# Moving four more k1 to Pool and reordering the loads around the first x of a fused FFT filter and feed-forward kernel

## The chip, the cores and the metric

The kernel runs on one core of one Trainium2 chip. The metric is the device time of one execution in microseconds (us); lower is better. Executions of one kernel agree within about 0.3%. A core has five engines that matter here: PE (TensorE, matmuls), DVE (VectorE), ACT (ScalarE), POOL (GpSimd) and SP (SyncE, which here only issues transfers), and 16 DMA engines. "PEld" in the profile is PE's weight load. In this kernel PE writes its results to banks of PSUM, a memory of the core, and VectorE or ScalarE brings them from there to the working memory, SBUF; this is called evacuation below.

## The reference

For each of 8 batches a sequence of 3008 positions with 256 channels is filtered in frequency, and the result goes through a two-layer feed-forward block:

```python
X = np.fft.rfft(x, axis=1)                      # x: (8, 3008, 256)
Y = X * (filt_r + 1j * filt_i)[None, :, :]
y = np.fft.irfft(Y, n=3008, axis=1)
h = y.reshape(24064, 256) @ w_in                # 256 -> 2048
out = np.maximum(0.01 * h, h) @ w_out           # 2048 -> 256
```

## The kernel before

The FFT is done by matmuls: 3008 = 94 x 32, so a first stage multiplies by a 94-point matrix, VectorE transposes, a second stage multiplies by one matrix for each of 24 frequencies k1 (`f2_sb`, three parts of 8), the filters are multiplied in, and two inverse stages follow (`inv2`, `i1_sb`). Later batches are woven into the feed-forward matmuls. The first batch has nothing to be woven into; its own code, the head, works on two halves of 128 channels.

```python
nc.sync.dma_start(small_sb[:], small_d.ap())
first_parts = ((0, 10), (10, 10), (20, 8), (28, 4))
for n0, nn in first_parts:
    x_load(0, n0, nn)                          # issued by Pool, float32 to float16 on the way
for hf in range(2):
    filt_load(fa_sb, filt_r, hf * DH, DH)      # two transfers each, issued by Pool
    filt_load(fb_sb, filt_i, hf * DH, DH)
    for i in (1, 0, 2) if hf == 0 else ():
        nc.gpsimd.dma_start(f2_sb[:, ts(i, NC // FP), :], f2_d.ap()[i])
nc.gpsimd.dma_start(w_in_sb[:], ...)
# ...
def first_s2(hf, c, n, kind, on_pool=False):   # second stage for k1 c to c+n-1
    ps = bank(kind, n, DH)                     # "pf": one of three PSUM banks, "ph": of two wide ones
    # ... n matmuls with f2_sb ...
    if on_pool:
        # act copies PSUM to SBUF (xs), which Pool reads
        # then 2 x n/4 products of 128x512 on gpsimd
    else:
        for i in range(2):
            nc.vector.tensor_tensor(y[i], ps, fs[i], AL.mult)
# ...
keep_warm(14)                                  # matmuls on zeros, meant to keep PE's clock up
# first stage, part by part of x, copies by dve and act in turn
t1_part(0, 0, True)(), t1_part(0, 1, True)()
upper(0, fa_sb, act), upper(0, fb_sb, dve)     # copy filters to the upper 64 partitions
first_s2(0, 8, 8, "ph", True)
t1_part(0, 2, True)()
first_s2(0, 0, 8, "ph")
# ... i1 load, next x load, t1_part(0, 3), upper(1, ...), and so on: see the diff
```

`upper(hf, fb_sb, dve)` copies one half of fb to the other partitions, on VectorE, and needs that half's filter loads; the products on VectorE stand behind it in program order.

Of the kernel before, what the change touches and what calls it, by code (L numbers as in the profile page):

```python
# [10 lines left out]
P = 128  # L11
# [8 lines left out]
NC = 24  # L20
Q = 32
R1 = 96
FP = 3
# [46 lines left out]
def kernel(  # L70
# [9 lines left out]
    nc = tc.nc  # L80
# [12 lines left out]
    f2_d = nc.inline_tensor(f2_np, name="fwd2_const")  # L93
# [4 lines left out]
    f2_sb = cpool.tile([P, NC, P], FP16, name="f2_sb")  # L98
    i1_sb = cpool.tile([P, N2, N1], FP16, name="i1_sb")
    small_sb = cpool.tile([P, 3, P], FP16, name="small_sb")  # L100
    fa_sb = cpool.tile([P, NC, D], FP16, name="fa_sb")
    fb_sb = cpool.tile([P, NC, D], FP16, name="fb_sb")
    w_in_sb = cpool.tile([P, NDT, DFF], FP16, name="w_in_sb")
# [17 lines left out]
    def bank(kind, n, w):  # L121
        of = wide if kind == "ph" else single
        t = of[turn[kind] % len(of)]
        turn[kind] += 1
        return t[:, : n * w].rearrange("p (n w) -> p n w", n=n)
# [5 lines left out]
    DH = D // 2  # L131

    def x_load(b, n0=0, nn=N2, d0=0, dn=D):

        for lo, cnt in ((0, R1),) if b + 1 < B else ((0, 64), (64, N1 - 64)):
            nc.gpsimd.dma_start(  # L136
                x_sb[lo : lo + cnt, ds(n0, nn), ds(d0, dn)],
                bass.AP(tensor=x.tensor, offset=x.offset + (b * N + lo * N2 + n0) * D + d0,
                        ap=[[N2 * D, cnt], [D, nn], [1, dn]]))

    def filt_load(dst, src, d0, dn):

        for q, first, sgn in ((0, 0, 1), (Q, N1, -1)):
            nc.gpsimd.dma_start(
                dst[q : q + Q, :, ds(d0, dn)],
                bass.AP(tensor=src.tensor, offset=src.offset + first * D + d0,
                        ap=[[N1 * D, N2 // 2], [sgn * NC * D, 2], [sgn * D, NC], [1, dn]]))


    nc.sync.dma_start(small_sb[:], small_d.ap())  # L150
    first_parts = ((0, 10), (10, 10), (20, 8), (28, 4))
    for n0, nn in first_parts:
        x_load(0, n0, nn)
    for hf in range(2):
        filt_load(fa_sb, filt_r, hf * DH, DH)
        filt_load(fb_sb, filt_i, hf * DH, DH)
        for i in (1, 0, 2) if hf == 0 else ():
            nc.gpsimd.dma_start(f2_sb[:, ts(i, NC // FP), :], f2_d.ap()[i])
    nc.gpsimd.dma_start(w_in_sb[:], moe_w_in.rearrange("(dt p) c -> p dt c", p=P))
    idle = cpool.tile([P, CH], FP16, name="idle")  # L160
    nc.vector.memset(idle[:], 0.0)

# [15 lines left out]
    def paired(t):  # L178
        return t[:].rearrange("p (e n t) -> p n e t", n=Q, t=2)

    def spread(dst, n0, ps, copy, e0=0):
        nn, de = ps.shape[1], ps.shape[2] // 2
        copy(paired(dst)[:, ds(n0, nn), ds(e0, de)], ps.rearrange("p n (e t) -> p n e t", t=2))  # L183
# [3 lines left out]
    def t1_part(b, i, flat=False):  # L187
        def go():
            a = big[(4 * b) % 3][:].bitcast(FP32)[:, ts(i, E4 * Q)].rearrange("p (e n) -> p e n", n=Q)
            o = big[(4 * b + 1) % 3][:].bitcast(FP32)  # L190
            if flat:
                o = o[:, ts(i, E4 * Q)].rearrange("p (e n) -> p e n", n=Q)
            else:
                o = o.rearrange("p (n e) -> p e n", n=Q)[:, ts(i, E4), :]
            nc.vector.transpose(o, a)  # L195
        return go
# [54 lines left out]
    def first_s1(n0, n, kind, copy):  # L251
        ps = bank(kind, n, D)
        for j in range(0, n, 2):
            nc.tensor.matmul(ps[:, ds(j, 2), :], fwd1[:N1], x_sb[:N1, ds(n0 + j, 2), :],  # L254
                             start=True, stop=True)
        spread(big[0], n0, ps, copy)
# [6 lines left out]
    def first_s2(hf, c, n, kind, on_pool=False):  # L263
        ps = bank(kind, n, DH)
        src = paired(big[1])
        for j in range(n):
            nc.tensor.matmul(ps[:, j, :].rearrange("p (e t) -> p e t", t=2), f2_sb[:, c + j, :],  # L267
                             src[:, c + j, ts(hf, DH // 2)], start=True, stop=True)
        fs = [f[:, ds(c, n), ts(hf, DH)] for f in (fa_sb, fb_sb)]
        y = [prods[hf][:, i, ds(c, n), :] for i in range(2)]  # L270
        if on_pool:
            xs = [scrp.tile([P, 4, DH], FP32, tag=f"p{j // 4 + 1}", name=f"fx_h{hf}_c{c + j}")
                  for j in range(0, n, 4)]
            for j, xf in enumerate(xs):
                act(xf[:], ps[:, ts(j, 4), :])
            for i in range(2):
                for j, xf in enumerate(xs):
                    nc.gpsimd.tensor_tensor(y[i][:, ts(j, 4), :], xf[:], fs[i][:, ts(j, 4), :], AL.mult)
# [4 lines that stand above are left out]
    def first_sa(hf, c, n=4):  # L283
        y = [prods[hf][:, i, ds(c, n), :] for i in range(2)]
        for j in range(0, n, 4):
            ps = bank("pf", 4, DH)
            for i, m in enumerate((inv2, inv2x)):
                nc.tensor.matmul(ps, m, y[i][:, ds(j, 4), :], start=(i == 0), stop=(i == 1))  # L288
            act(paired(big[2])[:, ds(c + j, 4), ts(hf, DH // 2)],
                ps.rearrange("p n (t e) -> p n e t", t=2))  # L290
# [19 lines left out]
    def upper(hf, t, copy):  # L310
        copy(t[64:P, :, ts(hf, DH)], t[0:64, :, ts(hf, DH)])


    def keep_warm(n):
        for _ in range(n):
            nc.tensor.matmul(po_ps.rearrange("p a d -> p (a d)"), idle[:, 0:P], idle[:],  # L316
                             start=True, stop=True)

    keep_warm(14)
    g = 0  # L320
    for n0, nn in first_parts:
        while nn:
            n = 2 if nn % 4 or n0 >= N2 - 4 else 4
            first_s1(n0, n, two[n // 4], (dve, act)[g % 2])
            n0, nn, g = n0 + n, nn - n, g + 1
        keep_warm(5 if n0 < N2 else 14)
    t1_part(0, 0, True)(), t1_part(0, 1, True)()
# [4 lines left out]

    nc.vector.memset(i1_sb[:, 0, 0:2], 0.0)
    nc.sync.dma_start(i1_sb[:], i1_d.ap())
    for n0 in (0, N2 // 2):
        x_load(1, n0, N2 // 2)
    t1_part(0, 3, True)()
    upper(1, fa_sb, act)
    first_s2(0, 16, 4, "pf"), first_s2(0, 20, 4, "pf")
    upper(1, fb_sb, dve)  # L340
    keep_warm(4)
    first_s2(1, 0, 8, "ph")
    first_sa(0, 0, 8)
    first_s2(1, 8, 8, "ph", True)
    nc.gpsimd.dma_start(w_out_sb[:], moe_w_out.rearrange("(ct p) d -> p ct d", p=P))
    first_sa(0, 16), first_sa(0, 20), first_sa(0, 8, 8)
    first_s2(1, 16, 4, "pf"), first_s2(1, 20, 4, "ph")
    first_sa(1, 0, 8)
    keep_warm(3)
# [81 lines left out]
    for slot in range(SL * (NCHUNK + 1)):  # L431
        ci, g = divmod(slot, SL)
# [36 lines left out]
```

## Time and profile before

The time before is 780.8 us, median of three runs. The profiled execution has a span of 778.8 us. Its first 39.36 us are the head; the rest is a PE-bound stretch.

| stretch | length | what PE, DVE and POOL are busy |
|---|---|---|
| 0 to 39.36 (head) | 39.36 us | 33.58, 29.04, 29.36 us |
| 39.36 to 778.8 (feed-forward) | 739.44 us | 734.88, 340.59, 119.36 us |

The table comes from the busy times in windows. PE is all but full in the second row (99% busy), so this stretch can hardly shrink, whatever the head does. In the first row no engine is full all the time: the head is a chain, and one reads it from the timeline and the chain of waits, which the prediction shows.

### The profile page before, as it was taken

Reading aid. Unit: us, or ns where it says so; the run is one execution under the profiler, and the core shown is the slowest. Engines: PE = TensorE matmul, PEld = TensorE weight load, DVE = VectorE, ACT = ScalarE, POOL = GpSimd, SP = SyncE. Lnnn points to the kernel's source line nnn. Section 1 sums busy time; section 2 is a strip of 40 time slices with the busy share of each in tenths; the row PEclk is TensorE's granted clock in tenths of the full one; section 3 lists DMA queues with packets and bytes.
Section 4 is the critical chain, followed back from the end, with each engine's and each line's share of the span. In section 5 each row is a group of like instructions: output and inputs, shape, how many; then the busy total and the mean of one; then the engine's idle time right before and its main releaser. Section 6 shows DMA issues by size and latency. Waiting matters only on the chain.

```text
span 778.8 us, 13329 instructions
## 1 busy us (share of the span) xinstructions
PE 768.5 (99%) x5688; PEld 521.5 (67%) x5688; DVE 369.6 (47%) x468; ACT 553.5 (71%) x784; POOL 148.7 (19%) x123
## 2 busy tenths in 40 slices
PE   8899999999999999999999999999999999999998
PEld 4556666666776676666777667666667667666666
DVE  5989742765238641576407743187523764200000
ACT  5777768676787768777686775967668676666663
POOL 6854200330005200042002410025000330000000
PEclk9999999999999999999999999999999999999999
DMA  9951013210151010510105010230101010110111
GB/s 186 227 92 56 28 41 71 66 42 29 41 108 42 28 41 28 116 35 28 42 28 122 28 41 29 53 96 28 41 28 42 28 38 31 41 42 28 41 41 55
DMA packets 36154, 43.36 MB, mean 56 GB/s; under 512 B 8130, under 2 KB 34370, under 8 KB 35330
## 3 DMA queue, kind: packets, MB, share of 16 engines
q0 software_dynamic: 10208, 17.01, 12.4%
q1 hardware_dynamic: 25888, 25.52, 9.3%
q8 instruction: 44, 0.72, 0.4%
q14 instruction: 14, 0.11, 0.1%
HBM read 34.10 MB, written 24.64 MB: 75 GB/s over the span
## 4 chain that ended last, share of the span: by engine, by line
PE 96%; DVE 2%; ACT 1%; DMA 1%; issue 0%; DVEq 0%; POOLq 0%
PE ph L377 41%; PE po_ps L391 41%; PE pf L173 3%; PE pf L241 2%; PE pf L213 2%; PE pf L229 2%; PE pf L391 1%; DMA x_sb<-in_x_dram 1%; DVE big L195 1%; DVE prod L281 1%; PE pf L288 0%; ACT big L183 0%; PE po_ps L316 0%; PE ph L267 0%; PE ph L254 0%
## 5 line engine op out<-in xcount | busy, mean ns | idle before, releaser
L382 ACT ACTIVATE gt_c<-ph 128x1024 f16<-128x1024 f32 x376 | 384.9, 1024 | 195.5 <-PE ph L377 193.4
L377 PE MATMUL ph<-yt,w_in_sb 128*128 128x512 f16 (+3 forms) x1600 | 386.6, 367 | 0.3
L391 PE MATMUL po_ps<-w_out_sb,gt_c 128*128 128x256 f16 x2944 | 381.5, 273 | 0.5 <-ACT ost_c_t L398 0.5
L391 PEld LDWEIGHTS <-gt_c 128*128 128x128 f16 x3008 | 290.5, 98 | 82.3 <-issue 2.4
L377 PEld LDWEIGHTS <-w_in_sb 128*128 128x128 f16 x1600 | 154.4, 98 | 97.5 <-issue 0.4
L222 POOL TENSOR_TENSOR y_b_g<-p_b_g,p_b_g 128x512 f16<-128x512 f32 x84 | 106.8, 1272 | 225.7 <-DVE p_b_g L220 225.7
L195 DVE STREAM_TRANSPOSE big<-big 128x1024 f32<-128x1024 f32 x32 | 56.0, 1846 | 126.0 <-ACT big L183 125.9
L183 ACT CAST big<-pf 128x512 f16<-128x512 f32 x186 | 106.6, 605 | 1.1 <-PE pf L254 1.1
L244 DVE CAST yt<-pf 128x376 f16<-128x376 f32 x112 | 56.4, 545 | 86.0 <-PE pf L241 86.0
L218 DVE TENSOR_TENSOR p_b_g<-pf,fa_sb 128x512 f32<-128x512 f32 x84 | 58.1, 692 | 38.3 <-PE pf L213 35.3
L398 ACT COPY ost_c_t<-po_ps 128x256 f32<-128x256 f32 x184 | 69.4, 377 | 6.6 <-PE po_ps L391 5.4
L203 DVE STREAM_TRANSPOSE big<-big 128x1024 f32<-128x1024 f32 x28 | 51.1, 1936 | 34.0 <-ACT big L183 34.0
L219 DVE TENSOR_TENSOR p_b_g<-pf,fb_sb 64x512 f32<-64x512 f32 x84 | 58.2, 692 | 1.1
L220 DVE TENSOR_TENSOR p_b_g<-pf,fb_sb 64x512 f32<-64x512 f32 x84 | 57.4, 683 | 1.1
L136 POOL DMA_DIRECT2D x_sb<-in_x_dram x13 | 7.1, 548 | 253.7 <-PE pf L173 252.9
L241 PEld LDWEIGHTS <-big 128*128 128x128 f16 x448 | 25.7, 98 | 13.2
L173 PE MATMUL pf<-x_sb,small_sb 94*128 94x512 f16 x112 | 33.6, 380 | 0.2 <-DVE yt L244 0.2
L213 PE MATMUL pf<-big,f_sb 128*128 128x256 f16 x168 | 32.1, 273 | 0.0
L229 PE MATMUL pf<-y_b_g,small_sb 128*128 128x512 f16 x84 | 31.9, 380 | 0.0
L213 PEld LDWEIGHTS <-f_sb 128*128 128x128 f16 x168 | 16.4, 98 | 19.7
L241 PE MATMUL pf<-i_sb,big 128*128 128x94 f16 x448 | 28.7, 206 | 0.0
L173 PEld LDWEIGHTS <-small_sb 94*128 94x128 f16 x112 | 10.7, 98 | 10.5
(50 smaller groups left out, 166.8 us busy)
## 6 DMA issues: line engine op xcount, KB each, us to landing
out_dram<-ost_c_t SPq DMA_DIRECT2D x92, 256.0 KB, 2.1
x_sb<-in_x_dram POOLq DMA_DIRECT2D x5, 1536.0 KB, 11.1
x_sb<-in_x_dram POOLq DMA_DIRECT2D x2, 768.0 KB, 12.1
x_sb<-in_x_dram POOLq DMA_DIRECT2D x3, 480.0 KB, 7.3
w_in_sb<-in_moe_w_in_dram POOLq DMA_DIRECT2D x1, 1024.0 KB, 13.3
w_out_sb<-in_moe_w_out_dram POOLq DMA_DIRECT2D x1, 1024.0 KB, 11.8
x_sb<-in_x_dram POOLq DMA_DIRECT2D x1, 1024.0 KB, 8.1
fa_sb<-in_filt_r_dram POOLq DMA_DIRECT2D x4, 192.0 KB, 8.5
```

Source lines behind the costliest of these rows:

```text
L173: nc.tensor.matmul(ps, fwd1[:N1], x_sb[:N1, ds(2 * g, 2), :], start=True, stop=True)
L183: copy(paired(dst)[:, ds(n0, nn), ds(e0, de)], ps.rearrange("p n (e t) -> p n e t", t=2))
L195: nc.vector.transpose(o, a)
L213: nc.tensor.matmul(ps[:, j, :], f2_sb[:, 2 * g + j, :], src[:, 2 * g + j, :], start=True, stop=True)
L218: nc.vector.tensor_tensor(p1[:], ps, fa, AL.mult)
L219: nc.vector.tensor_tensor(p2[0:64], ps[64:P], fb[64:P], AL.mult)
L222: nc.gpsimd.tensor_tensor(y1[:], p1[:], p2[:], AL.add)
L241: nc.tensor.matmul(ps[:, j, :], src[:, dt, n2, :], i1_sb[:, n2, :], start=True, stop=True)
L377: nc.tensor.matmul(ph[:, j, ds(o, ln)], w_in_sb[:, dt, ts(ct, P)], yt[:, dt, ds(lo, ln)], start=(dt == 0), stop=(dt == NDT - 1),)
L382: nc.scalar.activation(gts[ci][:, ds(2 * g, 2), :], ph, AF.Lrelu)
L391: nc.tensor.matmul(po, gts[ci][:, ct, ts(tj, P)], w_out_sb[:, ct, :], start=(ct == 0), stop=(ct == NCT - 1))
L398: nc.scalar.copy(ost[:, tj % 2, :], po)
```

## The change

The intent: VectorE bounds the head, so four more k1 of the first half (16 to 19) go to Pool, twelve in all. Two of the three second-stage matrices are sent by SP beside x. The filters are held back until x's second part is used, so that they don't compete with x: a one-element write by VectorE into the filter tile, behind the copy of first-stage group 4, makes the loads wait. The next x, and some orders on PE and ScalarE, move with this.

```diff
     nc.sync.dma_start(small_sb[:], small_d.ap())
+    for i in (1, 0):
+        nc.sync.dma_start(f2_sb[:, ts(i, NC // FP), :], f2_d.ap()[i])
     first_parts = ((0, 10), (10, 10), (20, 8), (28, 4))
     for n0, nn in first_parts:
         x_load(0, n0, nn)
-    for hf in range(2):
-        filt_load(fa_sb, filt_r, hf * DH, DH)
-        filt_load(fb_sb, filt_i, hf * DH, DH)
-        for i in (1, 0, 2) if hf == 0 else ():
-            nc.gpsimd.dma_start(f2_sb[:, ts(i, NC // FP), :], f2_d.ap()[i])
-    nc.gpsimd.dma_start(w_in_sb[:], moe_w_in.rearrange("(dt p) c -> p dt c", p=P))
 ...
-    keep_warm(14)
+    keep_warm(18)
 ...
             first_s1(n0, n, two[n // 4], (dve, act)[g % 2])
+            if g == 4:
+                nc.vector.memset(fa_sb[0:1, 0, 0:2], 0.0)
+                nc.vector.memset(f2_sb[0:1, NC - NC // FP, 0:2], 0.0)
+                for hf in range(2):
+                    filt_load(fa_sb, filt_r, hf * DH, DH)
+                    filt_load(fb_sb, filt_i, hf * DH, DH)
+                nc.sync.dma_start(f2_sb[:, ts(2, NC // FP), :], f2_d.ap()[2])
+                nc.gpsimd.dma_start(w_in_sb[:], moe_w_in.rearrange("(dt p) c -> p dt c", p=P))
 ...
     nc.sync.dma_start(i1_sb[:], i1_d.ap())
+    first_s2(0, 16, 4, "pf", True)
     for n0 in (0, N2 // 2):
         x_load(1, n0, N2 // 2)
     t1_part(0, 3, True)()
+    first_s2(0, 20, 4, "pf")
     upper(1, fa_sb, act)
-    first_s2(0, 16, 4, "pf"), first_s2(0, 20, 4, "pf")
     upper(1, fb_sb, dve)
     keep_warm(4)
+    first_s2(1, 8, 8, "ph", True)
     first_s2(1, 0, 8, "ph")
     first_sa(0, 0, 8)
-    first_s2(1, 8, 8, "ph", True)
     nc.gpsimd.dma_start(w_out_sb[:], ...)
-    first_sa(0, 16), first_sa(0, 20), first_sa(0, 8, 8)
+    first_sa(0, 20), first_sa(0, 8, 8), first_sa(0, 16)
```

Line numbers differ between the two kernels: what is L254, L267, L281, L288, L296, L311 and L377 before is L250, L263, L277, L284, L292, L307 and L383 in the changed one. Some of the experiments below have the head's numbers of before here.

## The prediction

> **What bounds the kernel now.** I read the page first. PE is busy for 99% of the span, and the chain that ended last is 96% PE, 82% of it the two matmul lines of the feed-forward stage (L377 and L391).
>
> ```profile
> span 778.8 us, 13329 instructions
> PE 768.5 (99%) x5688; PEld 521.5 (67%) x5688; DVE 369.6 (47%) x468; ACT 553.5 (71%) x784; POOL 148.7 (19%) x123
> PE 96%; DVE 2%; ACT 1%; DMA 1%; issue 0%; DVEq 0%; POOLq 0%
> ```
>
> The first line is the span, the second each engine's busy time, the third the chain's share by engine. The diff leaves everything behind the first batch's transform alone. In the timeline the first feed-forward matmul starts at 39.36 us, and from there PE runs without gaps. So some 740 us can't be moved, and what the change does to the start of L377 passes one to one into the time. The question is what sets that 39 us.
>
> I read the chain of waits for the first 62 us next (start, length, piece):
>
> ```profile
> 1.24 5.78 DMA x_sb<-in_x_dram
> 7.07 0.38 PE pf L254
> 13.61 0.45 PE pf L254 x2
> 14.77 2.38 DVE big L195 x2
> 18.15 1.25 DVE big L195
> 19.40 2.24 DVE prod L281 x2
> 21.64 1.18 DVE big L195
> 25.95 2.67 PE pf L288 x8
> 29.16 2.48 DVE prod L281 x4
> 31.65 2.29 DVE big L296 x2
> ```
>
> The head is: first x part (lands 7.03), stage one on PE with warming matmuls between, then VectorE from 14.77 to 33.94 with one excursion to PE and ScalarE. Its own timeline (start, length, instruction) shows only 0.61 us of idle in that stretch, before L281 at 29.16. VectorE is therefore the engine to relieve, and the intent to give four more k1 to Pool is aimed right. What decides is whether VectorE still gets its inputs in time:
>
> ```profile
> 12.38 0.74 POOL L144 DMA_DIRECT2D fa_sb<-in_filt_r_dram  x1 [0.45 <-DMA x_sb<-in_x_dram]
> 14.52 0.71 POOL L144 DMA_DIRECT2D fb_sb<-in_filt_i_dram  x1 [0.35 <-DMA fa_sb<-in_filt_r_dram]
> 16.94 1.33 POOL L159 DMA_DIRECT2D w_in_sb<-in_moe_w_in_dram  x1 [0.56 <-DMA fb_sb<-in_filt_i_dram]
> 17.17 0.95 DVE L311 COPY fb_sb<-fb_sb 64x3072 f16<-64x3072 f16 x1
> ```
>
> Pool's issues wait for landings eight transfers back, so they date the landings. The last x part landed at 12.38, both halves of the first-half fa by 14.52, fb's second by 16.94. VectorE's two transposes end at 17.14 and its copy of fb to the upper partitions starts at 17.17: fb came 0.2 us before it was needed. The windows show the DMA engines (the last three columns are PE clock, DMA share, GB/s):
>
> ```profile
> 4.50:11.00 6.50, 5.11 (x24) 2.18 (x23) 2.70 (x3) 2.16 (x3) 2.93 (x5) 1.00 1.05 205
> 11.00:15.25 4.25, 4.25 (x21) 1.91 (x20) 2.85 (x4) 2.79 (x4) 2.72 (x4) 1.00 1.80 181
> 15.25:17.25 2.00, 1.87 (x10) 0.67 (x9) 1.97 (x3) 2.00 (x1) 1.02 (x2) 1.00 1.15 390
> ```
>
> Four filter loads of 192 KB are 786 kB, which at 181 GB/s take 4.3 us: the second window is the filters of the first half. Before it runs x, behind it the second-stage matrices. So x isn't held up by the filters (they stand behind it in one queue), and the filters follow it without a gap. fb's landing, 16.94, is about 1.6 us after its bytes.
>
> **What the Trainium skill says.** "DMA: Bandwidth & Descriptors", section "Issuing engines are not separate DMA queues": transfers from different issuing engines share the same 16 DMA engines and interleave. So the matrices sent from SP beside x will take time from x; no run so far shows it. The same page, "Anatomy of one DMA", gives about 2 us of fixed cost, most of it the receipt; here it is 1.6 us from the last bytes of fb to its landing. "GPSIMD Engine Reference", "Elementwise — side-by-side cycle accounting", has a two-input add about 1.96 times slower than on VectorE; here the product of 128x512 takes 1.13 us on Pool (2.27 for two) against 0.67, 1.7 times, so the move is no loss where Pool is free. "TensorE: Matmul & The Clock Gate", "What's actually happening", has a free-running window of about 3.4 us of activity that sets half or full clock; the windows show a granted clock near 0.5 from about 24.3 to 27.7, behind PE's idle 20.86 to 22.86, which agrees.
>
> **The change, part by part.**
>
> Matrices beside x: 2 x 256 KB, at the 390 GB/s of the third window 1.35 us of the DMA engines. x's first part leaves them partly unused: 78 GB/s from 2.50 to 3.75, against 205 later, so of 1.25 us some 0.8 are free, and the SP transfers can start before x's first packets. I expect x 0.3 us later (choice: between 0 and 1). Stage one on PE follows x's first landing, so VectorE's first transpose goes from 14.77 to 15.1 and the two end at 17.45. The four more warming matmuls fill idle PE before x lands and cost nothing. Nothing is gained by having the matrices earlier, as their matmuls wait for those same transposes.
>
> Filters held back: the first filter issue now waits for a VectorE write behind the copy of stage-one group 4, which ends at 11.45 in the trace, 11.8 with the 0.3. From x's first issue (1.24) to its first packets (about 2.5) are 1.3 us, so filter bytes start at about 13.1 rather than 10.95, 2.1 us later; at 4.3 us for the four and the same receipt, fb lands at 16.94 + 2.1 = 19.0. The four issues at 0.72 us keep ahead of 1.08 us each. VectorE is ready at 17.45, so it stands idle for 1.55 us and its copy of fb starts at 19.05, 1.9 us later than before. ScalarE's copy of fa goes from 14.76 to 16.7 and ends at 19.45; Pool's products begin at about 20.05 (18.94 before).
>
> Twelve k1: VectorE loses two products of 128x512, 2 x 0.67 = 1.3 us. The last transpose of the first stage ended at 22.81; now 24.7. Then two products (1.3), the second copy (0.95) and the two large products (2.4) end at 29.5, against 28.56 before: +0.9. But the next products need L267's second-half k1 16 to 20, which stand on PE behind six groups of L288 in three PSUM banks. These now all come after Pool's second-half copies on ScalarE, where before two groups had gone ahead. Six evacuations of 0.59 from about 27.6: the fourth, which frees the bank, ends at 30.0, and the four matmuls (0.6) end at 30.6. Products start at 30.7 (29.16 before), and end at 33.2 against 31.65: +1.55.
>
> Pool: six products of 1.13 from 20.05 end at 26.9, x's next load is issued until 28.0, four products end at 32.6 (31.15 before). ScalarE's last evacuation before the second transposes then goes from 33.73 to about 35.2, the third transpose would have started at 35.5 anyway: beside the VectorE path, not on it. The next x lands around 37 and is needed at about 42; the input weights by about 28, needed at 41: hidden.
>
> Sum: +1.9 for filters (the 0.3 for x lies inside it: it postpones the release), -1.3 for the moved products, +0.95 given back to the wait for PE: +1.5 us. 780.8 + 1.5 = 782.3; I take 782.2, as the second half leaves VectorE some slack to recover.
>
> **The rivals.**
> First, the author's hope: filters in time, and VectorE's 1.3 us are gained, perhaps with the 0.6 us wait: 779 to 779.5. For it: VectorE is really the bound. Against: filters can't start before the release at 11.5, and 4.3 us of bytes plus 1.6 of receipt alone make 17.4 without any issue latency; the copy needs them at 17.45. It would take a latency near zero.
> Second, x pays in full for the matrices: 1.35 us instead of 0.3. Release and filters then move by another 1 us: 783.3. For it: the shared engines. Against: the unused share in x's first microsecond.
> Third, the wait passes to Pool or PE: ScalarE's fa copy, Pool's twelve and the half clock after PE's longer idle (20.5 to 24.7) hold the six L288 groups longer: at 2.67 us for eight cold matmuls against 1.73, up to 1 us more, 783.2. Against: clock windows lie where they lay, and the groups fall mostly behind 27.7.
> Fourth, everything is hidden: 780.8. Against: VectorE had 0.2 us of slack at the fb copy.
>
> **Range and chances.** The second and third rivals together give 784.2; filters 1 us quicker than I think, and the PE wait absent, give about 780.2. Runs of before spread by 1.4 us. 2% is 15.6 us, 40% of the whole head; no part comes near it.
>
> **What would show it.** In the changed profile: VectorE idle 1 to 2.5 us before L307 (the fb copy), released by the filter's DMA; first filter issue at about 11.8; x's first landing at 7.0 to 7.6; four filter loads at about 180 GB/s between 13 and 17.5; an idle of about 1.2 us before VectorE's second-half products of k1 16 to 20; the first feed-forward matmul at about 40.9. I am wrong if fb's copy starts before 18, if the release comes well before 11, or if the feed-forward stretch itself changes in length.

## The result

The changed kernel takes 784.43 us, median of four runs (784.32 to 785.36), against 780.9 for the kernel before in the same rounds. The ratio is 1.0051, with a 95% interval of 1.0033 to 1.0068: slower by half a per cent, clear of noise, and well within 2%. Ratios here are the mean time of one kernel's fast runs over that of the other's of the same rounds, so not quite the ratio of the medians. The predicted 782.2 has the right sign and less than half of the size; the measured time lies 0.2 us outside the range.

The kernel before has two groups of executions, which the record of its rounds beside the experiments shows (36 executions on three chips). In 17 the mean granted clock was 0.999 to 1.0 and the time 779.52 to 780.07 us; in 19 it was 0.997 or 0.998 and the time 780.35 to 781.03: about 0.8 us more. A clock of 0.50 for 3.4 us, as in its profile, lowers the mean to 0.998, so the groups are with and without such a stretch. A ratio near 1 therefore has to be read at equal clock.

The profiled execution is the slowest of the four, so its span is 4.8 us longer than that of before, where the medians differ by 3.5. First the page of the changed kernel (span; PE's row; the chain's shares):

```profile
span 783.6 us, 13345 instructions
PE 771.1 (98%) x5692; PEld 522.8 (67%) x5692; DVE 369.5 (47%) x468; ACT 554.2 (71%) x785; POOL 148.9 (19%) x122
PE 94%; DMA 2%; DVE 2%; ACT 1%; issue 0%; POOL 0%; DVEq 0%; POOLq 0%
```

PE gave up 2% of the chain, and DMA's share rose. The feed-forward stretch is 739.28 us long (739.44 before), so the whole loss is in the head: the first feed-forward matmul starts at 44.32 us instead of 39.36. The chain of waits of the changed kernel in its first 62 us (start, length, piece) says where:

```profile
1.94 8.21 DMA x_sb<-in_x_dram
...
12.66 1.44 POOL fa_sb L144 x2
...
14.79 6.37 DMA fb_sb<-in_filt_i_dram
...
22.24 1.25 DVE big L191
23.48 2.24 DVE prod L277 x2
25.72 1.19 DVE big L191
26.95 1.93 PE ph L263 x16
28.88 4.68 PE pf L284 x12
33.56 0.45 PE pf L263 x4
34.10 2.49 DVE prod L277 x4
```

The kernel before had VectorE's two transposes here, at 14.77, with no filter load in the chain at all. Now the chain goes from x through Pool's issues to the landing of fb at 21.2, and only then to VectorE. The timeline of VectorE in the changed kernel (start, length, instruction, and in brackets the idle time before it and what ended it):

```profile
12.28 0.06 DVE L323 MEMSET fa_sb<- 1x1 uint32 x1
...
15.65 2.37 DVE L191 STREAM_TRANSPOSE big<-big 128x1024 f32<-128x1024 f32 x2 [0.20 <-ACT big L179]
21.25 0.96 DVE L307 COPY fb_sb<-fb_sb 64x3072 f16<-64x3072 f16 x1 [3.22 <-DMA fb_sb<-in_filt_i_dram]
...
28.10 1.96 DVE L307 COPY fb_sb<-fb_sb 64x3072 f16<-64x3072 f16 x1
...
34.10 0.69 DVE L277 TENSOR_TENSOR prod<-pf,fa_sb 128x512 f16<-128x512 f32 x1 [1.66 <-PE pf L263]
```

The kernel before, for comparison:

```profile
25.21 0.95 DVE L311 COPY fb_sb<-fb_sb 64x3072 f16<-64x3072 f16 x1
29.16 0.69 DVE L281 TENSOR_TENSOR prod<-pf,fa_sb 128x512 f16<-128x512 f32 x1 [0.61 <-PE pf L267]
```

Four things are to be seen. The transposes start 0.88 us later than before. The first fb copy starts at 21.25 instead of 17.17, after 3.22 us of idle for the filter's DMA. The second fb copy takes 1.96 us, where both took 0.95 before. And the products of the second half wait 1.66 us for PE instead of 0.61. The windows of the changed kernel (busy time and count by engine, then PE clock, DMA share and GB/s; the share is not capped at 1) show the transfers and the clock:

```profile
12.00:14.50 2.50, 2.50 (x13) 1.09 (x12) 1.57 (x4) 1.54 (x2) 1.84 (x3) 1.00 0.48 102
15.25:19.00 3.75, 3.63 (x22) 2.05 (x21) 2.57 (x3) 0.37 (x1) 3.75 (x6) 1.00 1.60 153
20.00:24.00 4.00, 1.75 (x12) 1.01 (x10) 2.72 (x3) 3.93 (x5) 1.49 (x2) 1.00 1.82 183
26.40:33.00 6.60, 6.04 (x27) 3.26 (x28) 5.99 (x6) 3.49 (x6) 6.59 (x8) 0.50 1.02 253
```

Two windows of the kernel before:

```profile
12.00:14.50 2.50, 2.50 (x13) 1.09 (x12) 1.87 (x2) 1.46 (x2) 1.47 (x2) 1.00 1.82 179
24.30:27.70 3.40, 3.40 (x16) 1.77 (x14) 3.34 (x5) 2.78 (x6) 1.26 (x2) 0.50 1.03 279
```

In the first of the four, where the kernel before moved its filters at 179 GB/s, the DMA share is 0.48 instead of 1.82. In the second the first half's filters are moved, at 153 GB/s; in the third the second half's, at 183. In the fourth PE's granted clock is 0.50 for 6.6 us (3.4 us before), and it follows 5.2 us of idle (2.0 before).

### The profile page after: what moved, and what is told of

Read it like the earlier page. It is cut to its first block, busy times and chain, and to the rows that moved or that the text cites. A ratio compares the mean times of both kernels' runs of the same rounds, so it can differ in the third digit from the quotient of the medians.

```text
span 783.6 us, 13345 instructions
## 1 busy us (share of the span) xinstructions
PE 771.1 (98%) x5692; PEld 522.8 (67%) x5692; DVE 369.5 (47%) x468; ACT 554.2 (71%) x785; POOL 148.9 (19%) x122
## 4 chain that ended last, share of the span: by engine, by line
PE 94%; DMA 2%; DVE 2%; ACT 1%; issue 0%; POOL 0%; DVEq 0%; POOLq 0%
PE ph L383 41%; PE po_ps L397 41%; PE pf L169 3%; PE pf L237 2%; PE pf L209 2%; PE pf L225 2%; DMA x_sb<-in_x_dram 1%; PE pf L397 1%; DMA fb_sb<-in_filt_i_dram 1%; DVE prod L277 1%; PE pf L284 1%; ACT big L179 0%; DVE big L191 0%; DVE big L292 0%; PE ph L301 0%
## 5 line engine op out<-in xcount | busy, mean ns | idle before, releaser
L383 PE MATMUL ph<-yt,w_in_sb 128*128 128x512 f16 (+3 forms) x1600 | 386.4, 366 | 0.3
L383 PEld LDWEIGHTS <-w_in_sb 128*128 128x128 f16 x1600 | 154.5, 98 | 97.4 <-issue 0.4
L225 PE MATMUL pf<-y_b_g,small_sb 128*128 128x512 f16 x84 | 31.8, 379 | 0.0
```

The lines of the kernel that those rows point to most:

```text
L383: nc.tensor.matmul(ph[:, j, ds(o, ln)], w_in_sb[:, dt, ts(ct, P)], yt[:, dt, ds(lo, ln)], start=(dt == 0), stop=(dt == NDT - 1),)
```

## The experiments

My theory after the result: the late release of the filters carries nearly all of the loss; beside it, twelve k1 give back in a slower copy and a longer wait for PE what they save. The rivals: the matrices beside x, or the twelve k1 and their order, are what costs. All eleven kernels gave correct results and were timed in five rounds beside the kernel before. The table sums up what the sections below use; all but the last two columns are from the timelines of single profiled runs (us).

| kernel | first transpose | first fb copy | second fb copy takes | idle before second-half products | first feed-forward matmul | median | ratio |
|---|---|---|---|---|---|---|---|
| before | 14.77 | 17.17 | 0.95 | 0.61 | 39.36 | - | 1 |
| changed | 15.65 | 21.25 | 1.96 | 1.66 | 44.32 | 784.43 | 1.0051 |
| loads_alone | 15.64 | 20.89 | 0.95 | 0.96 | 43.44 | 784.51 | 1.0059 |
| twelve_alone | 14.75 | 17.16 | 1.37 | 1.61 | 39.57 | 780.56 | 1.0004 |
| no_hold | 15.78 | 18.39 | 1.14 | 1.89 | 40.87 | 781.46 | 1.0013 |
| early_release | 15.30 | 18.63 | 1.54 | 1.92 | 41.54 | 781.81 | 1.0019 |
| after_warm | 15.39 | 21.33 | 1.67 | none | 42.51 | 783.35 | 1.0040 |
| hf1_late | 15.57 | 20.36 | 1.51 | 1.38 | 42.82 | 783.85 | 1.0049 |
| third_on_pool | 15.62 | 22.52 | 0.96 | 1.21 | 44.41 | 785.25 | 1.0061 |
| twelve_s2_early | 14.73 | 17.13 | 1.38 | none | 39.11 | 780.35 | 1.0001 |
| twelve_s2_warm | 14.62 | 17.02 | 1.37 | none | 38.98 | 780.21 | 1.0001 |
| twelve_wide | 14.61 | 17.01 | 1.37 | none | 37.98 | 779.33 | 0.9987 |
| twelve_wide_x | 14.59 | 17.00 | 1.13 | none | 37.58 | 779.24 | 0.9985 |

### loads_alone: the loads of the change, the computing of before

Against the changed kernel:

```diff
-    first_s2(0, 16, 4, "pf", True)
 ...
-    first_s2(0, 20, 4, "pf")
     upper(1, fa_sb, act)
+    first_s2(0, 16, 4, "pf"), first_s2(0, 20, 4, "pf")
     upper(1, fb_sb, dve)
 ... (the order of before in first_s2(1, 8, ...) and first_sa(0, ...) as well)
```

> The new loads (matrices on SP beside x, filters held) with the computing order and the eight k1 on Pool of the kernel before. Theory A: the late filters carry the loss. VectorE's first copy of fb then starts at about 21.2 us as in the changed kernel (17.17 before), its last first-stage transpose ends at about 26.9, the second copy of fb takes 0.95 us again because no Pool product lies beside it, and the first feed-forward matmul starts 4.1 to 5.2 us later than before (43.5 to 44.5 us): ratio 1.005 to 1.0065. Rival B: a good part of the loss is the twelve k1 and the new order (a copy of 1.96 us instead of 0.95, 1.66 us of waiting for PE): then the loads alone cost some 2 us less than the whole change, ratio about 1.002 to 1.003.

The median is 784.51 us, the ratio 1.0059 (1.0047 to 1.0072). The loads alone cost as much as the whole change. VectorE's two fb copies and the products behind the wait, in its timeline:

```profile
20.89 0.95 DVE L307 COPY fb_sb<-fb_sb 64x3072 f16<-64x3072 f16 x1 [2.88 <-DMA fb_sb<-in_filt_i_dram]
...
28.93 0.95 DVE L307 COPY fb_sb<-fb_sb 64x3072 f16<-64x3072 f16 x1
...
33.24 0.69 DVE L277 TENSOR_TENSOR prod<-pf,fa_sb 128x512 f16<-128x512 f32 x1 [0.96 <-PE pf L263]
```

The idle time for the filter is there without the twelve k1, and the first feed-forward matmul is 4.08 us late. Theory A holds; the rival, which expected a ratio of 1.002 to 1.003, falls.

### twelve_alone: twelve k1 and the new order, the loads of before

Against the kernel before, the edit is the last part of the change's diff, from `first_s2(0, 16, 4, "pf", True)` on.

> The loads of the kernel before with the twelve k1 on Pool and the new computing order. Theory A: VectorE is saved two products (1.34 us), but its second copy of fb falls beside Pool's products of k1 16 to 19 and takes about 1.9 us instead of 0.95, and the second-half products of k1 16 to 20 wait about 1 us for PE instead of 0.6; in sum -0.3 to +0.5 us, ratio 0.9995 to 1.001. Rival B: the whole 1.3 us is gained, ratio about 0.998. Rival C: order and Pool cost 1 us or more, ratio above 1.0015.

The median is 780.56 us, the ratio 1.0004 (0.9991 to 1.0016). This is no measurable change, as theory A said: two products of 0.67 us left VectorE and nothing was gained. (All five executions are at a clock of 0.997 or 0.998; their mean, 780.45, is within 0.15 us of that of the half-clock group of before in the same rounds, 780.58.) VectorE's timeline and Pool's say why:

```profile
24.00 1.37 DVE L311 COPY fb_sb<-fb_sb 64x3072 f16<-64x3072 f16 x1
...
29.37 0.69 DVE L281 TENSOR_TENSOR prod<-pf,fa_sb 128x512 f16<-128x512 f32 x1 [1.61 <-PE pf L267]
```

```profile
23.40 1.15 POOL L278 TENSOR_TENSOR prod<-fx_h_c,fa_sb 128x512 f16<-128x512 f32 x1
24.52 1.87 POOL L278 TENSOR_TENSOR prod<-fx_h_c,fb_sb 128x512 f16<-128x512 f32 x1
```

Of the 1.34 us saved, 0.42 went into the second fb copy (1.37 instead of 0.95) and 1.0 into the wait for PE (1.61 instead of 0.61): +0.1 us. Theory A had both parts, with other sizes: 1.9 for the copy and about 1 for the wait. The copy starts while a Pool product runs and ends 0.82 us after that product's end, about 24.55. The Pool product that starts during the copy takes 1.87 us instead of 1.15. The two instructions behave as if they took turns. The other runs fit: where no Pool product lies beside the copy (before, loads_alone), it takes 0.95; where one started with it (the changed kernel, Pool's product at 28.09), it takes 1.96, nearly the product's 1.15 and its own time in a row. In all ten runs in which a Pool product was under way when the second copy started, the copy ends 0.81 or 0.82 us after that product. Pool's issuing of loads meets it too: the issue of the input weights beside the first copy of the kernel before takes 1.33 us, where it takes 0.72 in twelve_alone. VectorE's products, which read PSUM, kept their 1.2 us beside Pool's. The Trainium skill names a cause that would do this: "GPSIMD Engine Reference", section "1. Specifications", has Pool's SBUF interfaces shared with VectorE, with contention for VectorE instructions in a two-port mode or with two SBUF inputs. The traces show the delay; that this copy uses such a mode, no run shows.

### no_hold: filters directly behind x again

```diff
+    for hf in range(2):
+        filt_load(fa_sb, filt_r, hf * DH, DH)
+        filt_load(fb_sb, filt_i, hf * DH, DH)
+    nc.gpsimd.dma_start(w_in_sb[:], ...)          # behind the x loads
 ...
             if g == 4:
-                nc.vector.memset(fa_sb[0:1, 0, 0:2], 0.0)
-                (the filter and w_in loads)
```

> The changed kernel with the filters and input weights issued directly behind x again; matrices stay on SP, twelve k1 stay. Theory A (the hold is the cause): filter bytes follow x's without a gap, fb lands at about 17.8, VectorE's first copy of fb starts at 18.0 to 18.3, about 0.9 us later than before (what x pays for the matrices) instead of 4.1; the head loses 0.5 to 1.5 us against before, ratio 1.0005 to 1.002. Rival B: the matrices beside x or the twelve k1 cost most: ratio stays at 1.004 or more.

The median is 781.46 us, the ratio 1.0013 (1.0000 to 1.0026). VectorE's timeline at the first copy:

```profile
18.39 0.96 DVE L311 COPY fb_sb<-fb_sb 64x3072 f16<-64x3072 f16 x1 [0.24 <-DMA fb_sb<-in_filt_i_dram]
```

Taking away the hold takes away 3.0 us of the idle time, and 0.0038 of the ratio. Theory A holds: the hold is most of the loss. It brought x nothing that shows, as the first transpose starts at 15.65 with it and at 15.78 without. What is left against twelve_alone is put down to the matrices beside x: first transpose 15.78 against 14.75, medians 781.46 against 780.56, so about 0.9 to 1.0 us. The two ratios' intervals overlap, but the first transpose starts at 15.30 to 15.78 in all seven profiles with the matrices on SP and at 14.59 to 14.77 in all six without.

### early_release: the hold ends with group 0 instead of 4

```diff
-            if g == 4:
+            if g == 0:
                 nc.vector.memset(fa_sb[0:1, 0, 0:2], 0.0)
                 (the filter and w_in loads)
+            if g == 4:
                 nc.vector.memset(f2_sb[0:1, NC - NC // FP, 0:2], 0.0)
                 nc.sync.dma_start(f2_sb[:, ts(2, NC // FP), :], f2_d.ap()[2])
```

> The changed kernel with the filters released behind stage-one group 0 rather than 4 (about 8.9 us instead of 12.3); the third matrix stays behind group 4. Theory A: it is the time of the release and the latency behind it: filters are queued when x's bytes end at about 12.2, so fb lands at 17.7 to 18.7 and the time is that of the kernel with no hold within 0.5 us. Rival B: the slower filter transfer (about 155 instead of 181 GB/s, with Pool issuing without a pause) or something else about the hold matters more than its time: fb's copy at 19.5 or later, ratio 1.003 or more.

The median is 781.81 us, the ratio 1.0019 (1.0005 to 1.0033): that of no_hold within its interval. Pool's first filter issue is at 8.94 us, before x's bytes have ended, and the filters run at 175 GB/s between 12.2 and 15.5. So a hold costs little if it ends while x is still being moved (VectorE is idle for the filter for 0.96 us, 0.24 in no_hold); what costs is the time of the release.

### after_warm: more warming matmuls in PE's idle stretch

```diff
-    keep_warm(4)
+    keep_warm(26)
```

> The changed kernel with 26 instead of 4 warming matmuls in PE's long idle stretch (21.7 to 26.9 us), 22 x 0.216 = 4.8 us of work nobody waits for. Theory A: the second-half products of k1 16 to 20 wait 1.66 us because PE runs its 12 L284 matmuls at half clock (4.86 us); at full clock they are paced by ScalarE (6 evacuations of 0.6, about 3.6 us), the wait falls to 0.3 to 0.8 us, the time by 0.9 to 1.3 us, ratio about 1.004. Rival B: order and banks make the wait, not the clock: wait and time as in the changed kernel, ratio 1.005 to 1.006.

The median is 783.35 us, the ratio 1.0040 (1.0027 to 1.0052). PE's and VectorE's timelines:

```profile
28.78 2.94 PE L284 MATMUL pf<-prod,small_sb 128*128 128x512 f16 x12
```

```profile
32.30 0.69 DVE L277 TENSOR_TENSOR prod<-pf,fa_sb 128x512 f16<-128x512 f32 x1
```

The granted clock is 1.00 throughout, twelve L284 matmuls take 2.94 us instead of 4.86, and VectorE's 1.66 us of waiting are gone altogether. Theory A holds: the wait in the changed kernel comes of PE's half clock, and about 1 us (1.1 in the medians) goes with it, though the intervals of the two ratios overlap. It isn't a cost of the late filters alone: twelve_alone, whose filters came in time and whose half clock lasted about 3.4 us, has nearly the same wait, 1.61 us. The wait needs both, the order with the twelve k1 (0.61 us in the order of before) and the half clock.

### hf1_late: only four filter loads at the release

```diff
             (at the release: the first half's loads alone)
     t1_part(0, 0, True)()
+    nc.vector.memset(fa_sb[0:1, 0, DH : DH + 2], 0.0)
+    (the second half's filter loads and w_in)
     t1_part(0, 1, True)()
```

> The changed kernel with the second half's filter loads and the input weights released only behind VectorE's first transpose, so that Pool issues four loads and then pauses, while the first half's bytes are moved. Theory A: filter packets move at 145 to 165 GB/s while Pool issues without a pause, and at 180 when it doesn't: from about 15.7 us on 180 GB/s, fb of the first half lands at about 20.5 instead of 21.2, the time falls by 0.5 to 0.7 us, ratio about 1.0045. Rival B: the rate has nothing to do with Pool's issuing (in the early release run it was 170 to 178 while Pool issued): rate and landing as in the changed kernel, ratio 1.005 to 1.006.

The median is 783.85 us, the ratio 1.0049 (1.0035 to 1.0063). The first fb copy starts at 20.36, so 0.9 us earlier than in the changed kernel, but the rate is 159 GB/s between 14.7 and 17.0, where Pool issues for only 0.71 us, and 163 in the next 2 us, where it issues nearly all the time. The time gained fits theory A; its rate, 180 GB/s where Pool pauses, did not come. The rate stayed near the changed kernel's 153, as rival B had it, but B's landing did not. The interval doesn't separate this run's time from the changed kernel's.

### third_on_pool: nothing between release and filters

```diff
                 for hf in range(2):
                     filt_load(fa_sb, filt_r, hf * DH, DH)
                     filt_load(fb_sb, filt_i, hf * DH, DH)
-                nc.sync.dma_start(f2_sb[:, ts(2, NC // FP), :], f2_d.ap()[2])
+                    if hf == 0:
+                        nc.gpsimd.dma_start(f2_sb[:, ts(2, NC // FP), :], f2_d.ap()[2])
```

> The changed kernel with the third matrix taken from SP and issued by Pool behind the first half's filters, so that nothing else is moved between the release and the first filter bytes. In the changed kernel those follow Pool's first issue (12.66) by about 2.0 us, and SP's matrix is moved from 13.3 to 14.7, just before them. Theory A: that matrix holds them back, and mixes with them: filter bytes then start at 13.9 to 14.2 and run nearer 180 GB/s, fb's copy starts at 20.0 to 20.6 (21.25 in the changed kernel), ratio 1.0035 to 1.0045. Rival B: the latency and the low rate (153 GB/s) are the filters' own: bytes start at 14.6 or later, fb's copy at 21.0 to 21.5, ratio 1.005 to 1.006.

The median is 785.25 us, the ratio 1.0061 (1.0047 to 1.0074). This is a miss for theory A on all but one point, and the landing misses rival B (21.0 to 21.5) too. The first filter bytes do come earlier, between 14.00 and 14.25 (1.4 to 1.6 us behind Pool's issue at 12.62). But the rate is no better:

```profile
15.25:19.00 3.75, 3.62 (x22) 2.04 (x21) 2.53 (x3) 0.97 (x2) 3.75 (x7) 1.00 1.52 144
```

fb's copy starts at 22.52, 1.3 us later than in the changed kernel, although the bytes started earlier. So the SP matrix isn't what makes the rate low. What does stays open: in the five profiles in which the filters were issued into an empty queue, their first half was moved at 135 (after_warm, 14.5 to 19.0), 144, 145 (loads_alone, 14.7 to 19.0), 153 and 159 GB/s (the windows differ, and some hold the start of the transfer), and in the three in which they stood ready behind x (before, no_hold, early_release) at 181, 181 and 175.

### twelve_s2_early and twelve_s2_warm: can the moved products be turned into time?

From here the loads are those of before. Against twelve_alone, the second half's matmuls of k1 16 to 23 go ahead of four groups on PE; the second of the two kernels also has `keep_warm(12)` instead of 4.

```diff
     first_sa(0, 0, 8)
+    first_s2(1, 16, 4, "pf"), first_s2(1, 20, 4, "ph")
 ...
     first_sa(0, 20), first_sa(0, 8, 8), first_sa(0, 16)
-    first_s2(1, 16, 4, "pf"), first_s2(1, 20, 4, "ph")
```

> The loads of the kernel before, twelve k1 on Pool, and the second half's matmuls of k1 16 to 23 moved on PE from behind six L288 groups to behind two. Theory A: the 1.61 us that VectorE waits for PE in the twelve-k1 run comes from that order; it goes, VectorE's products end at about 30.2 instead of 31.8, Pool's last products (31.9) then hold the third transpose a little; first feed-forward matmul at 38.2 to 38.8, ratio 0.998 to 0.9987. Rival B: Pool or ScalarE takes over as the bound at once, nothing gained: ratio 0.9995 to 1.001.

> The same with 12 instead of 4 warming matmuls in PE's idle stretch (20.8 to 22.9 us). Theory A: PE keeps its full clock from 24 to 28 us and the L288 groups end up to 1 us earlier; as VectorE no longer waits for them, the gain over the run without is 0 to 0.3 us. Rival B: PE's half clock still carries the path: 0.5 us or more below the run without.

The medians are 780.35 and 780.21 us, both ratios 1.0001 (0.9989 to 1.0014). Nothing is gained, as rival B said of the first; warming adds nothing measurable, as theory A said of the second, although its executions are all at a clock of 0.999 to 1.0. VectorE no longer waits for PE and is through with its products at 30.1, 1.5 us earlier than before. But now PE waits for VectorE (PE's timeline of twelve_s2_early):

```profile
29.00 1.89 PE L288 MATMUL pf<-prod,small_sb 128*128 128x512 f16 x8 [1.04 <-DVE prod L281]
```

The k1 moved forward hold one of the three single PSUM banks until VectorE has multiplied them; PE's next groups need that bank, ScalarE's evacuations slip behind them, and VectorE's last transposes then wait for ScalarE (0.63 and 1.03 us). The wait had only changed hands.

### twelve_wide and twelve_wide_x: the same in a wide bank

```diff
     first_sa(0, 0, 8)
+    first_s2(1, 16, 8, "ph")
 ...
-    first_s2(1, 16, 4, "pf"), first_s2(1, 20, 4, "ph")
```

By the code, the wide bank is free by then because ScalarE, not VectorE, empties the one that the Pool k1 used. `keep_warm(12)` stays. The second kernel also issues the next x's second half behind Pool's second-half products.

> The loads of the kernel before, twelve k1 on Pool, 12 warming matmuls in PE's idle stretch, and the second half's k1 16 to 23 moved behind two L288 groups into one wide PSUM bank instead of a single and a wide one. In the two runs with that move in single banks VectorE no longer waited for PE, but PE (1.0 to 1.6 us before L288) and then ScalarE waited for the bank that VectorE still held. Theory A: with the single banks free, ScalarE's six evacuations run on from 25.1 to about 29, both last transposes start earlier, Pool's last product (31.9) sets the third: first feed-forward matmul 0.5 to 0.9 us before that of the kernel before, ratio 0.9988 to 0.9995. Rival B: Pool's chain (31.9) and the ScalarE evacuations behind it hold the end where it was: ratio 0.9996 to 1.0005.

> The same with the second half of the next x load issued behind Pool's second-half products instead of before them, which takes 0.55 us out of Pool's chain. If Pool sets the third last transpose, this gains up to another 0.5 us (ratio 0.998 to 0.999); if the next x then comes late (its second half is first needed about 45 us), the feed-forward's first chunk shows waits on it and nothing is gained.

The medians are 779.33 and 779.24 us against 780.6 for the kernel before in the same rounds, with ratios of 0.9987 (0.9973 to 1.0000) and 0.9985 (0.9973 to 0.9998). These are the fastest kernels, by a small margin: the first's interval touches 1, the second's just excludes it. In the profile the first feed-forward matmul starts at 37.98 and 37.58 us instead of 39.36. What VectorE now waits for in twelve_wide, before its last two transposes:

```profile
32.93 2.37 DVE L296 STREAM_TRANSPOSE big<-big 128x1024 f32<-128x1024 f32 x2 [0.78 <-ACT big L289]
```

This is the chain through Pool's last product, which ends about 31.8, and ScalarE's last evacuation. With Pool relieved of one issue (twelve_wide_x) the idle time falls to 0.47. The step between these two is 0.09 us in the medians and can't be told from noise. The first is a little better than theory A expected (0.9988 to 0.9995); the second lies inside what was expected (0.998 to 0.999).

How much of the 1.3 us do the twelve k1 earn? All ten executions of these two kernels are at a clock of 0.999 to 1.0, and of the kernel before in the same rounds only three of nine. Those three have a mean of 779.82 us, against 779.32 and 779.18 here: at equal clock 0.5 and 0.6 us. The rest of the difference is the clock. The run that would separate the two, the kernel before with `keep_warm(12)` and nothing else, was not made. What the bank did is clearer: twelve_wide and twelve_s2_warm have the same loads, the same twelve k1, the same warming and the same clock, and their medians, from different rounds, differ by 0.9 us.

## Why the prediction was wrong

**What bounds the kernel: right.** The loss is all in the head, and the feed-forward stretch kept its length within 0.2 us. The filters' landing before VectorE's first fb copy is the step that decides, and the idle time predicted there appeared there. Loads_alone adds the loads alone and has the whole loss; no_hold takes the hold away, and most of the loss goes; twelve_alone has neither.

**The step that failed is "Filters held back": +1.9 us predicted, +4.08 measured** (first fb copy 17.17 to 21.25). The mechanism was right, the size off in three of its four terms:

| term | predicted | measured in the changed kernel | missed by |
|---|---|---|---|
| release (VectorE's write done) | 11.8 | 12.34 | +0.5 |
| release to first filter bytes | 1.3 | about 2.3 (0.3 to Pool's issue at 12.66, then bytes from about 14.65) | +1.0 |
| four loads | 4.3 at 181 GB/s | 5.1 (786 kB at 153 GB/s) | +0.8 |
| last byte to fb copy | 1.6 | about 1.5 (19.8 to 21.25) | -0.1 |

The sum of the last column is the 2.2 us between the predicted 19.05 and the measured 21.25. The release was late because x paid more for the matrices (next point). The latency had been taken from x's first load, about 1.3 us from issue to bytes, and Pool's own reaction to the release had been left out; third_on_pool, where the bytes start about 0.5 us sooner, points to the third matrix, which SP moved in the same gap, for that part; this is one profile, and the windows do not tell the bytes of two transfers apart. The rate had been taken from loads that stood ready in the queue; loads released late are slower in each of five profiles, for a reason that stays open.

**Matrices beside x: 0.3 us predicted for x, 0.67 measured at its first matmul (7.07 to 7.74) and 0.88 at the first transpose.** The argument from unused DMA time in x's first microsecond was too hopeful. No_hold against twelve_alone puts the whole price at about 1 us, between this and the rival that charged x the full 1.35.

**Twelve k1: the saving of 1.3 us and the longer wait were right in kind.** Predicted idle before the second-half products was 1.2 us, measured 1.66 in the changed kernel. The order was only half of its cause: at full clock the wait vanishes (after_warm). The third rival had named the half clock and set it aside, since the clock windows of before would lie where they lay; they did not, and the half clock lasted 6.6 us instead of 3.4. The second fb copy's 1.0 us beside Pool's product was not foreseen at all.

**The sum.** Predicted: 1.9 - 1.3 + 0.95 = 1.5 us. Measured in the profile, at the end of VectorE's products (31.65 to 36.59): 4.08 for the first copy, -1.34 for the moved products, +1.01 for the second copy, +1.05 for the wait, together 4.8, and 0.1 of small gaps. The range, whose upper end added the second and third rivals, let the filters slip by 1 us more only through x; that their latency and rate could be worse than those of before, together 1.8 us, was not in it.

**The author's rival (779 to 779.5) fell with these loads.** Its premise, that VectorE's 1.3 us are there to be had, is borne out in part at most: at equal clock twelve_wide and twelve_wide_x gain 0.5 and 0.6 us.

## What to carry to other kernels

Before holding a load back, ask whether it was really competing: here the filters stood behind x in the same queue, cost it nothing that shows, and were needed 0.2 us after they landed. Holding them cost their whole start-up again. When work is moved off the engine that bounds, look at what then holds its inputs, PSUM banks included: of five kernels with the same four k1 moved and the loads of before, three gained nothing. And before a small gain is put down to an edit, compare executions at equal clock: warming alone may be what was gained.

## What the Trainium skill lacked or had wrong

- "DMA: Bandwidth & Descriptors" gives about 1 us to the first byte of a Pool-issued transfer. Here, counted from the start of Pool's issue instruction, it was about 1.3 us for x (issue at 1.24, bytes from 2.50), about 2.0 for the held filters beside an SP transfer, and 1.4 to 1.6 without one.
- The same page does not say that Pool-issued loads in small pieces run slower when issued into an empty queue than when they stand ready in it: 135 to 159 GB/s in five profiles against 175 to 181 in three. The cause is open.
